# Gated linear attention and a soft mixture of experts: stages of one tile form side by side on TensorE, turns of 112 columns, and another order at the start and the end

## The chip, the cores and the metric

The program runs on one core of one Trainium2 chip. The metric is the device time of one execution in microseconds (us), the median of several runs. Everything is float32.

## The reference

```python
f = 1.0 / (1.0 + np.exp(-f_logit))
for t in range(S):                       # S = 768, for each of B = 4, H = 8, D = 48
    state = f[:, :, t, :, None] * state + np.einsum('bhd,bhe->bhde', k[:, :, t], v[:, :, t])
    y[:, :, t] = np.einsum('bhd,bhde->bhe', q[:, :, t], state)
x = y.transpose(0, 2, 1, 3).reshape(B * S, H * D)              # 3072 x 384
logits = x @ phi                                               # 32 slots, 4 for each of 8 experts
d = softmax of logits over the 3072 tokens;   slot_input = d.T @ x
slot_out[e] = np.maximum(slot_input[e] @ w1[e], 0.0) @ w2[e]   # 384 -> 1024 -> 384
c = softmax of logits over the 32 slots;      out = c @ slot_out
```

## The kernel before

**Units.** The attention is cut into 12 units (NU): 6 chunks of 128 time steps, for each two batches at a time. A unit holds 16 heads, two beside each other on the partitions (rows 0 to 47 and 64 to 111), so eight head pairs of 128 columns; `w` is 0 or 1 for the first or last four of them. Unit u carries a state on to unit u + 2.

For a unit, ACT makes exp(-f) and ln(1 + ...) in place (`d_exp`, `d_ln`, L179 to L184), DVE scans it along time (`d_scan`, L189), and ACT makes the two exponentials p and g of it (`d_p` L192, `d_g` L198; g is written over f). POOL multiplies k by g (`d_k`, L202) and q by p (`d_q`, L206). `d_pend` (L209) keeps the last column of p.

TensorE then has these stages: the turns of k (`kt`, L215, eight transposes into PC, copied by ACT in `kt_copy`, L218); the scores of each half (`scores`, L226, into PD, masked and copied by DVE in `s_mask`, L229); kv (L244, k times v into PC, to which DVE adds the state, L251, and which it scales into the next state, L254); inter (L266, state times q into PB); intra for each half (L275, v times scores into PB). ACT copies PB out (`y_copy`, L287). `x_tr` (L295) turns that into PA, and `x_copy` brings it out, the first half by ACT (L300), the second by DVE (L301). PA, PB, PC and PD are all the PSUM there is, two banks each.

**Groups.** Two units make a group g of 512 tokens: `c_lg` (L313) makes their logits in PA, `c_max` (DVE, L323) the running maximum, `c_exp` the exponential et and the copy lt (ACT), `c_tr` turns both (L337), `c_copy` (DVE, L341) brings them into el, `c_pin` (L350) multiplies et with x into the second bank of PA, and `c_join` (DVE, L354) adds it to pin.

**End.** `t_max` and `t_max2` bring the maxima of the four partition groups together, `t_psi` (L400) makes the slot inputs, `up` (L408, w1 with relu on ACT) and `turn` (L414, with a masking product on DVE, L415) run four times, `t_z` (L420) makes the sums, `c_soft` and `c_soft2` the softmax over slots on DVE, `c_ct` (L443) turns it, `down` (L448) multiplies by w2 in 16 steps for each half h of the output columns, `slot_out` and `slot_out2` (L455, L460) add up over experts and copy to s4, `combine` (L472) makes the output, copied by ACT and DVE (L475) and stored in six DMAs (L478). `flag` looks whether p and exp stayed in range; if not, a slower general part would run. `warm` (L151) is a product of ones whose result is not used.

**Order.** The order is written out by hand: `at(t, fn, ...)` gives each stage a planned time (unit length T, offsets OFF), the stages are sorted by it, and every engine runs its own in that order. Each load is issued by SP in the same order, eight at most in flight. The buffers are rings: f three, p two, k and q three, v three, x three. w1 is loaded all along, w2 into the rings of f, p, k, q and v as they come free at the end.

The forms in which TensorE is used are: scores 48 rows x 128 columns (two at once), turns 128 x 128, kv and intra 128 x 48 (two at once), inter 48 x 48 (four), lg, pin, up and down 128 x 32 (four).

## Time and profile before

| | us |
|---|---|
| timed runs | 181.41, 182.70, 182.75; median 182.7 |
| profiled execution | 180.49 |
| its span, first to last instruction | 178.8 |
| TensorE busy | 154.9 (87% of the span) |
| DVE busy | 105.0 (59%) |
| ACT busy | 92.5 (52%) |
| POOL busy | 56.9 (32%) |

The profile is that of one execution. Busy time is an average over stages: the units fill the span from about 10 to 123 us, the end the rest. Where TensorE is busy nearly all the time, its own stream of work sets the pace; where it is not, one has to look at which wait ends last. The granted clock is the share of TensorE's full 2.4 GHz that it got in a stretch; 0.5 is its lower level of 1.2 GHz. The 1.7 us between the span and the time of the execution lie outside of the instructions.

### The profile page before, as it was taken

What the parts mean: (1) busy time and instruction counts of PE and PEld (TensorE: products, weight loads), DVE (VectorE), ACT (ScalarE), POOL (GpSimd) and SP (SyncE); (2) the same over time, 40 slices, a digit from 0 to 9 for tenths busy, and PEclk for the clock granted to TensorE, in tenths of its full rate; (3) what the DMA queues carried; (4) which work ended last, traced back from release to release, by engine and by line L of the source; (5) the groups of instructions that cost most, each with busy time, mean ns of one, the idle gap of its engine ahead of it and who ended that gap; (6) DMA issues with size and microseconds to landing.
All of it is one profiled execution on the core that took longest, in us unless ns stands there. A gap on an engine that the chain in (4) does not pass through costs nothing. (4 is left out here: it accounts for less than half of the span.)

```text
span 178.8 us, 5442 instructions
## 1 busy us (share of the span) xinstructions
PE 154.9 (87%) x2396; PEld 116.5 (65%) x2396; DVE 105.0 (59%) x140; ACT 92.5 (52%) x156; POOL 56.9 (32%) x43
## 2 busy tenths in 40 slices
PE   7858599999999999999999999999898899898600
PEld 7747498878787878877787787767533346464400
DVE  6588266678787777777869677273424822225420
ACT  5965991858767595939493956402303112023410
POOL 2324846290909072725555374500000000000000
PEclk9999756999999999999999999999999999999955
DMA  4999999999299958999797948199978992009690
GB/s 140 324 406 414 408 410 409 391 312 405 67 414 396 391 201 262 369 415 330 279 363 231 341 143 343 28 408 421 419 313 282 423 423 110 5 5 368 266 406 33
DMA packets 12849, 53.97 MB, mean 302 GB/s; under 512 B 1425, under 2 KB 1553, under 8 KB 12817
## 3 DMA queue, kind: packets, MB, share of 16 engines
q1 hardware_dynamic: 12816, 53.55, 78.3%
q8 instruction: 20, 0.33, 0.7%
q14 instruction: 13, 0.10, 0.2%
HBM read 48.82 MB, written 4.72 MB: 300 GB/s over the span
## 5 line engine op out<-in xcount | busy, mean ns | idle before, releaser
L206 POOL TENSOR_TENSOR arena<-arena 128x1024 f32<-128x1024 f32 (+1 forms) x12 | 26.3, 2189 | 45.2 <-ACT arena L192 40.1
L229 DVE TENSOR_TENSOR arena<-pd,mask 128x1024 f32<-128x1024 f32 x24 | 29.3, 1223 | 18.6 <-PE pd L226 18.4
L202 POOL TENSOR_TENSOR arena<-arena 128x1024 f32<-128x1024 f32 (+1 forms) x14 | 29.5, 2112 | 11.5 <-DMA arena<-in_k_dram 5.8
L226 PE MATMUL pd<-arena 48*128 48x128 f32 x384 | 29.7, 297 | 3.2 <-DVE arena L206 2.5
L189 DVE TENSOR_TENSOR_SCAN arena<-again,arena 128x1024 f32<-128x1024 f32 (+1 forms) x14 | 29.5, 2110 | 4.7 <-ACT arena L184 4.6
L226 PEld LDWEIGHTS pd<-arena 48*128 48x128 f32 x384 | 25.0, 199 | 10.1 <-issue 5.0
L275 PE MATMUL pb<-arena 128*48 128x128 f32 x384 | 26.0, 281 | 0.0
L275 PEld LDWEIGHTS pb<-arena 128*48 128x48 f32 x384 | 20.5, 125 | 3.7 <-issue 3.5
L218 ACT COPY arena<-pc 128x768 f32<-128x768 f32 x10 | 8.0, 800 | 19.0 <-PE pc L215 19.0
L192 ACT ACTIVATE arena<-arena 128x1024 f32<-128x1024 f32 (+1 forms) x14 | 13.2, 940 | 2.7 <-DVE arena L189 2.7
L181 ACT ACTIVATE arena<-arena 128x1024 f32<-128x1024 f32 (+1 forms) x14 | 12.9, 924 | 2.1 <-DMA arena<-in_f_dram 2.1
L215 PE MATMUL pc<-ident,arena 128*128 128x128 f32 x80 | 11.6, 288 | 2.8 <-POOL arena L202 2.7
L295 PE MATMUL pa<-ident,arena 128*128 128x128 f32 x96 | 14.0, 292 | 0.0
L198 ACT ACTIVATE arena<-arena 128x1024 f32<-128x1024 f32 (+1 forms) x14 | 13.1, 936 | 0.5
L184 ACT ACTIVATE arena<-arena 128x1024 f32<-128x1024 f32 (+1 forms) x14 | 13.1, 934 | 0.4
L287 ACT COPY arena<-pb 128x1024 f32<-128x1024 f32 x11 | 11.2, 1017 | 2.3 <-PE pb L275 2.3
L300 ACT COPY arena<-pa 128x384 f32<-128x384 f32 x12 | 5.7, 478 | 12.8 <-PE pa L295 12.8
L215 PEld LDWEIGHTS pc<-ident,arena 128*128 128x128 f32 x80 | 8.8, 145 | 5.1 <-POOL arena L202 3.8
L295 PEld LDWEIGHTS pa<-ident,arena 128*128 128x128 f32 x96 | 11.0, 148 | 1.6 <-issue 0.4
L266 PE MATMUL pb<-arena 48*48 48x128 f32 x320 | 10.9, 274 | 0.0
L448 PE MATMUL pd<-arena 128*32 128x192 f32 x144 | 9.2, 330 | 1.0 <-DVE sob L455 0.6
L301 DVE COPY arena<-pa 128x384 f32<-128x384 f32 x12 | 6.7, 558 | 5.7 <-ACT arena L300 5.7
(123 smaller groups left out, 195.9 us busy)
## 6 DMA issues: line engine op xcount, KB each, us to landing
wr<-in_w_dram SPq DMA_DIRECT2D x23, 768.0 KB, 7.7
arena<-in_w_dram SPq DMA_DIRECT2D x9, 768.0 KB, 9.7
arena<-in_k_dram SPq DMA_DIRECT2D x12, 512.0 KB, 5.5
arena<-in_q_dram SPq DMA_DIRECT2D x12, 512.0 KB, 6.8
arena<-in_f_dram SPq DMA_DIRECT2D x10, 512.0 KB, 7.1
arena<-in_v_dram SPq DMA_DIRECT2D x12, 384.0 KB, 6.2
out_dram<-wr SPq DMA_DIRECT2D x6, 768.0 KB, 4.2
arena<-in_f_dram SPq DMA_DIRECT2D x4, 256.0 KB, 4.8
```

Of the source, the lines that this page charges most:

```text
L181: nc.scalar.activation(cols(R("f", u), h), cols(R("f", u), h), AF.Exp, scale=-1.0, accum_out=a)
L184: nc.scalar.activation(cols(R("f", u), h), cols(R("f", u), h), AF.Ln, bias=1.0)
L189: nc.vector.tensor_tensor_scan(t, cols(again, h), t, 0.0, op0=ALU.mult, op1=ALU.add)
L192: nc.scalar.activation(cols(R("p", u), h), cols(R("f", u), h), AF.Exp, scale=-1.0)
L198: nc.scalar.activation(cols(G(u), h), cols(R("f", u), h), AF.Exp)
L202: (eng or nc.gpsimd).tensor_tensor(t, t, cols(G(u), h), op=ALU.mult)
L206: (eng or nc.gpsimd).tensor_tensor(t, t, cols(R("p", u), h), op=ALU.mult)
L215: nc.tensor.transpose(PC[:, a // 4, 128 * (a % 4) : 128 * (a % 4) + 128], kq[:, a], ident)
L226: nc.tensor.matmul(PD[:, r, 128 * p : 128 * p + 128], kq[rs, 4 * w + p], qq[rs, 4 * w + p], start=True, stop=True)
L229: nc.vector.tensor_tensor(heads(R("sc", w), L), PD.rearrange("p r (a t) -> p (r a) t", t=L), mask.unsqueeze(1).broadcast_to([128, 8, L]), ...
L275: nc.tensor.matmul(ys[o : o + D, 4 * w + p], vb(u, 4 * w + p, r ^ w), sc[:, r, p], start=u < 2 and p == 0, stop=p == 3, skip_group_check=True,
L295: nc.tensor.transpose(PA[:, w, 128 * p : 128 * p + 128], xTs[u][:, w, p], ident)
```

## The change

The planned unit length and all offsets are new, and so is the sequence: what follows is the order on the engines. The diff without the table and lists of order:

```diff
+W = 64 + 48
-    NF, NP_, NK, NQ, NVB, NX = 3, 2, 3, 3, 3, 3
+    NF, NP_, NK, NQ, NVB, NX = 3, 2, 3, 3, 2, 4
...
-            nc.tensor.transpose(PC[:, a // 4, 128 * (a % 4) : 128 * (a % 4) + 128], kq[:, a], ident)
+            nc.tensor.transpose(PC[:, a // 4, 128 * (a % 4) : 128 * (a % 4) + W], kq[:W, a], ident[:W, :W])
...
+    def SP(u, w):
+
+        return PA if u == 0 and w else PD
...
-                nc.tensor.matmul(PD[:, r, 128 * p : 128 * p + 128], kq[rs, 4 * w + p], qq[rs, 4 * w + p], start=True, stop=True)
+                nc.tensor.matmul(SP(u, w)[:, r, 128 * p : 128 * p + 128], kq[rs, 4 * w + p], qq[rs, 4 * w + p], start=True, stop=True)
...
-            nc.vector.tensor_copy(t[:, 1], PB[:, 1])
+
+    def y_last(u):
+        t = xTs[u].rearrange("p n a t -> p n (a t)")
+        nc.scalar.copy(t[:, 1, :256], PB[:, 1, :256])
+        nc.vector.tensor_copy(t[:, 1, 256:], PB[:, 1, 256:])
...
-                nc.tensor.transpose(PA[:, w, 128 * p : 128 * p + 128], xTs[u][:, w, p], ident)
+                nc.tensor.transpose(PA[:, w, 128 * p : 128 * p + W], xTs[u][:W, w, p], ident[:W, :W])
...
-        return (PA if g < NV - 1 else PC)[:, 1]
+        return PB[:, 0] if g < NV - 1 else PC[:, 1]
...
-    FIN = [(PA, PC), (PB, PA), (PC, PB)]
+    FIN = [[(PA, PC), (PB, PA), (PC, PB)], [(PA, PB), (PC, PD), (PA, PB)]]
...
-        items = [(t_psi,), (warm, 1), (up, 0, 0), (c_exp, NV - 1, (1,)), (c_tr, NV - 1, (1,)), (c_copy, NV - 1, (1,)), (c_soft,), (up, 0, 1), (turn, 0, 0)]
-        items += [(c_soft2,), (up, 1, 0), (turn, 0, 1), (t_z,), (up, 1, 1), (turn, 1, 0)]
+        items = [(t_psi,), (c_exp, NV - 1, (1,)), (t_zs,), (up, 0, 0), (up, 0, 1), (c_tr, NV - 1, (1,)), (turn, 0, 0), (c_copy, NV - 1, (1,))]
+        items += [(up, 1, 0), (turn, 0, 1), (t_z,), (c_soft,), (up, 1, 1)]
...
+        items += [(down, 0, *STEPS[x]) for x in range(8)]
+        items += [(turn, 1, 0), (turn, 1, 1), (c_soft2,), (flag,)]
+        for x in range(8, 16):
+            items.append((down, 0, *STEPS[x]))
+        items += [(slot_out, 0), (c_ct, 0), (c_ct, 1), (flag_2,)]
+        items += [(down, 1, *STEPS[x]) for x in range(2)]
...
-        (y_copy, NU - 1), (warm, 2), (c_lg, NV - 1), (x_tr, NU - 1), (c_max, NV - 1), (x_copy, NU - 1), (warm, 2),
-        (c_exp, NV - 1, (0,)), (c_tr, NV - 1, (0,)), (c_copy, NV - 1, (0,)), (t_max,), (warm, 1), (t_max2,),
-        (c_pin, NV - 1), (c_join, NV - 1), (warm, 2),
+        (y_last, NU - 1), (c_lg, NV - 1), (x_tr, NU - 1), (c_max, NV - 1), (c_exp, NV - 1, (0,)), (t_max,), (c_tr, NV - 1, (0,)),
+        (c_copy, NV - 1, (0,)), (x_copy, NU - 1), (t_max2,), (warm, 1), (c_pin, NV - 1), (c_join, NV - 1), (warm, 1),
```

Of y of the last unit, the first bank is now copied by ACT behind the first intra stage, and the second in two halves by `y_last`. `t_zs` makes zs, which was the first line of `t_z`; `flag_2` holds what was the second half of `flag`.

**The first place** is the middle of the program, units 4 and 5. On TensorE before (L226 scores, L244 kv, L266 inter, L295 turns of x, L275 intra, L313 logits, L215 turns of k, L337 turns of et and lt):

```order
L226 MATMUL pd<-arena 128x128 x8
L244 MATMUL pc<-arena 48x48 x16
L266 MATMUL pb<-arena 48x128 x16
L226 MATMUL pd<-arena 128x128 x8
L295 MATMUL pa<-ident,arena 128x128 x8
L275 MATMUL pb<-arena 48x128 x8
L313 MATMUL pa<-arena,phs 32x128 x16
L215 MATMUL pc<-ident,arena 128x128 x8
L275 MATMUL pb<-arena 48x128 x8
L226 MATMUL pd<-arena 128x128 x8
L337 MATMUL pa<-ident,et 128x128
L337 MATMUL pa<-ident,lt 128x128
```

On TensorE now, the same place (L232 scores, L217 turns of k, L305 turns of x, L362 pin, L325 logits, L272 inter, L250 kv, L281 intra, L349 turns of et and lt):

```order
L232 MATMUL pd<-arena 128x128 x8
L217 MATMUL pc<-ident,arena 128x112 x8
L305 MATMUL pa<-ident,arena 128x112 x8
L232 MATMUL pd<-arena 128x128 x8
L362 MATMUL pa<-arena,el 32x384 x4
L325 MATMUL pa<-arena,phs 32x128 x16
L272 MATMUL pb<-arena 48x128 x16
L250 MATMUL pc<-arena 48x48 x16
L281 MATMUL pb<-arena 48x128 x16
L232 MATMUL pd<-arena 128x128 x8
L217 MATMUL pc<-ident,arena 128x112 x8
L305 MATMUL pa<-ident,arena 128x112 x8
```

The turns of k stand with those of x (and in odd units with those of et and lt, which now go to PB), pin stands with the logits, kv with both intra stages; a unit is finished before the next begins.

On ACT before, in such a unit (L287 y, L192 p, L198 g, L181 exp, L184 ln, L209 last column of p, L300 x, L218 copy of the turned k):

```order
L287 COPY arena<-pb 128x1024
L192 ACTIVATE arena<-arena 128x1024
L198 ACTIVATE arena<-arena 128x1024
L181 ACTIVATE arena,check<-arena 128x1024
L184 ACTIVATE arena<-arena 128x1024
L209 COPY check<-arena 128x8
L300 COPY arena<-pa 128x384
L218 COPY arena<-pc 128x768
```

On ACT now (L293 y, L194 p, L220 copy of the turned k, L311 x, L200 g, L211, L183 exp, L186 ln):

```order
L293 COPY arena<-pb 128x1024
L194 ACTIVATE arena<-arena 128x1024
L220 COPY arena<-pc 128x768
L311 COPY arena<-pa 128x384
L200 ACTIVATE arena<-arena 128x1024
L211 COPY check<-arena 128x8
L183 ACTIVATE arena,check<-arena 128x1024
L186 ACTIVATE arena<-arena 128x1024
```

The copies of k and x have moved between p and g of the next unit. DVE, which before had the scan behind the copy of x, now has it behind the second mask and both state products.

**The second place** is unit 2 on DVE. Before (L229 mask, L254 state, L301 x, L189 scan):

```order
L189 SCALAR_TENSOR_TENSOR arena<-again,arena 128x1024
L229 TENSOR_TENSOR arena<-pd,mask 128x1024
L254 TENSOR_TENSOR arena<-pc,check 128x384
L229 TENSOR_TENSOR arena<-pd,mask 128x1024
L301 COPY arena<-pa 128x384
L189 SCALAR_TENSOR_TENSOR arena<-again,arena 128x1024
L229 TENSOR_TENSOR arena<-pd,mask 128x1024
```

Now (L235 mask, L191 scan, L313 x, L260 state):

```order
L235 TENSOR_TENSOR arena<-pd,mask 128x1024
L191 SCALAR_TENSOR_TENSOR arena<-again,arena 128x512 x2
L313 COPY arena<-pa 128x384
L235 TENSOR_TENSOR arena<-pd,mask 128x1024
L260 TENSOR_TENSOR arena<-pc,check 128x384
L191 SCALAR_TENSOR_TENSOR arena<-again,arena 128x1024
L235 TENSOR_TENSOR arena<-pd,mask 128x1024
```

The first row is now the first mask of unit 1; unit 2 is scanned in halves behind it, and the scan of unit 3 stands ahead of the first mask of unit 2 (last two rows). In the start besides, all four half products of k and q of unit 0 are on DVE (those of k were on POOL), units 1 and 2 have their products in halves on POOL, q ahead of k, both scores of unit 0 stand together, and the loads of k and f of the next units have moved ahead of v.

**The third place** is the end on TensorE. Before (L400 psi, L408 up, L337 turn of lt, L414 turn, L420 sums, L448 down):

```order
L400 MATMUL pd<-wd,pin 32x32 x12
L151 MATMUL pc<-ones 128x128
L408 MATMUL pa<-wr,et 32x512 x12
L337 MATMUL pc<-ident,lt 128x128
L408 MATMUL pa<-wr,et 32x512 x12
L414 MATMUL pb<-ident,arena 128x128 x4
L408 MATMUL pc<-wr,et 32x512 x12
L414 MATMUL pb<-ident,arena 128x128 x4
L420 MATMUL pd<-small,same 128x1
L408 MATMUL pc<-wr,et 32x512 x12
L414 MATMUL pb<-ident,arena 128x128 x4
L448 MATMUL pd<-arena 32x192 x12
```

Now (L412 psi, L420 up, L349 turn of lt, L426 turn, L434 sums, L462 down, L457 `c_ct`):

```order
L412 MATMUL pd<-wd,pin 32x32 x12
L420 MATMUL pa<-wr,et 32x512 x24
L349 MATMUL pc<-ident,lt 128x128
L426 MATMUL pb<-ident,arena 128x128 x4
L420 MATMUL pc<-wr,et 32x512 x12
L426 MATMUL pb<-ident,arena 128x128 x4
L434 MATMUL pd<-small,same 128x1
L420 MATMUL pc<-wr,et 32x512 x12
L462 MATMUL pd<-arena 32x192 x32
L426 MATMUL pb<-ident,arena 128x128 x8
L462 MATMUL pd<-arena 32x192 x32
L457 MATMUL pc<-ident,el 128x128 x6
```

The first two up stages stand together, the last two turns stand together in the middle of the first 16 down steps, and `c_ct` behind them. Two instead of four down steps of the second half stand ahead of `slot_out2`, and the others are spread 4, 4, 4, 2 instead of 4, 3, 3, 2 from there on.

## Rows read from the trace of the kernel before

**Rows 1.** The view that gives each engine's busy time (number of instructions) in stretches of the span, with granted clock, share of the DMA engines and GB/s; us from the span's start.
```profile
18.00:22.00 4.00, 2.20 (x12) 1.63 (x14) 0.65 (x1) 3.77 (x7) 3.54 (x3) 0.72 1.02 406
22.00:27.00 5.00, 4.99 (x63) 4.41 (x61) 3.37 (x3) 4.52 (x7) 2.14 (x1) 0.50 1.02 412
27.00:32.00 5.00, 5.00 (x43) 4.30 (x44) 3.75 (x3) 0.92 (x2) 2.53 (x2) 0.70 1.03 411
...
51.00:70.00 19.00, 18.66 (x336) 15.09 (x334) 14.48 (x18) 13.63 (x23) 9.40 (x4) 1.00 0.87 331
```

**Rows 2.** TensorE's timeline in the middle, most of a period of two units (start, us from the first start to the last end, line, what, number of instructions, [idle before <- releaser]; a stage's 8 matmuls of two passes are 16 instructions, a turn is one).
```profile
51.32 1.16 PE L226 MATMUL pd<-arena 48*128 48x128 f32 x16
52.41 0.92 PE L244 MATMUL pc<-arena 128*48 128x48 f32 x32
53.27 1.09 PE L266 MATMUL pb<-arena 48*48 48x128 f32 x32
...
57.74 1.08 PE L313 MATMUL pa<-arena,phs 128*32 128x128 f32 x32 [0.26 <-DVE arena L301]
58.76 1.09 PE L215 MATMUL pc<-ident,arena 128*128 128x128 f32 x8
59.78 1.08 PE L275 MATMUL pb<-arena 128*48 128x128 f32 x16
60.79 1.16 PE L226 MATMUL pd<-arena 48*128 48x128 f32 x16
...
64.23 0.85 PE L350 MATMUL pa<-arena,el 128*32 128x384 f32 x8
...
70.28 1.16 PE L226 MATMUL pd<-arena 48*128 48x128 f32 x16
```

**Rows 3.** TensorE's timeline again: two intra stages that stand together and the score stage behind them; then two short cuts out of one stage of turns, for the pace of its instructions.
```profile
105.06 1.95 PE L275 MATMUL pb<-arena 128*48 128x128 f32 x32
106.94 1.16 PE L226 MATMUL pd<-arena 48*128 48x128 f32 x16
...
47.42 0.71 PE L295 MATMUL pa<-ident,arena 128*128 128x128 f32 x5
...
47.53 0.38 PE L295 MATMUL pa<-ident,arena 128*128 128x128 f32 x2
```

**Rows 4.** Groups of instructions by line and form, of TensorE's weight loads (number, busy us, mean ns of one, idle before).
```profile
L215 PEld LDWEIGHTS pc<-ident,arena 128*128 128x128 f32 x80 | 8.8, 145 | 5.1 <-POOL arena L202 3.8 <-issue 1.2
L244 PEld LDWEIGHTS pc<-arena 128*48 128x48 f32 x320 | 8.6, 131 | 1.4 <-issue 0.5 <-ACT arena L181 0.2 <-DMA arena<-in_q_dram 0.2
```

**Rows 5.** The same view, of DVE and ACT.
```profile
L229 DVE TENSOR_TENSOR arena<-pd,mask 128x1024 f32<-128x1024 f32 x24 | 29.3, 1223 | 18.6 <-PE pd L226 18.4
...
L189 DVE TENSOR_TENSOR_SCAN arena<-again,arena 128x1024 f32<-128x1024 f32 x10 | 24.7, 2466 | 4.1 <-ACT arena L184 4.1
...
L192 ACT ACTIVATE arena<-arena 128x1024 f32<-128x1024 f32 x10 | 10.7, 1067 | 0.8 <-DVE arena L189 0.8
...
L218 ACT COPY arena<-pc 128x768 f32<-128x768 f32 x10 | 8.0, 800 | 19.0 <-PE pc L215 19.0
...
L300 ACT COPY arena<-pa 128x384 f32<-128x384 f32 x12 | 5.7, 478 | 12.8 <-PE pa L295 12.8
...
L301 DVE COPY arena<-pa 128x384 f32<-128x384 f32 x12 | 6.7, 558 | 5.7 <-ACT arena L300 5.7
...
L251 DVE TENSOR_TENSOR pc<-pc,arena 128x384 f32<-128x384 f32 x8 | 4.5, 561 | 0.3
```

**Rows 6.** ACT's timeline in one unit, from exp to the op behind ln.
```profile
64.41 1.04 ACT L181 ACTIVATE arena<-arena 128x1024 f32<-128x1024 f32 x1
...
65.58 1.06 ACT L184 ACTIVATE arena<-arena 128x1024 f32<-128x1024 f32 x1
66.54 0.19 ACT L209 COPY check<-arena 128x8 f32<-128x8 f32 x1
```

**Rows 7.** Timelines of the start, of DVE (first row) and of TensorE.
```profile
8.78 2.40 DVE L206 TENSOR_TENSOR arena<-arena 128x512 f32<-128x512 f32 x2 [1.45 <-ACT check L209]
...
10.68 1.16 PE L226 MATMUL pd<-arena 48*128 48x128 f32 x16 [2.47 <-DVE arena L206]
...
17.91 0.66 PE L215 MATMUL pc<-ident,arena 128*128 128x128 f32 x4 [0.91 <-POOL arena L202]
20.37 1.12 PE L215 MATMUL pc<-ident,arena 128*128 128x128 f32 x4 [1.80 <-POOL arena L202]
...
41.93 1.16 PE L226 MATMUL pd<-arena 48*128 48x128 f32 x16
```

**Rows 8.** TensorE's timeline from the end of the last unit's intra stages to the last combine.
```profile
122.58 0.71 PE L151 MATMUL pc<-ones 128*128 128x128 f32 x4
...
131.04 2.78 PE L408 MATMUL pa<-wr,et 128*32 128x512 f32 x24
134.78 0.33 PE L337 MATMUL pc<-ident,lt 128*128 128x128 f32 x1 [0.95 <-ACT lt L333]
...
142.55 0.38 PE L420 MATMUL pd<-small,same 128*128 128x1 f32 x2 [0.85 <-DVE small L419]
...
155.92 0.59 PE L460 MATMUL pd<-sob,same 128*128 128x192 f32 x2
...
169.07 0.43 PE L472 MATMUL pb<-s,ct 32*128 32x192 f32 x2 [0.59 <-ACT wr L475]
```

More of the change, by code (lines that the diff above doesn't have):

```diff
@@ L551, in gla_soft_moe_kernel @@
     done0 = ("kt", "ktok", "sc0", "sc1", "mask0", "mask1", "intra0", "intra1", "kv", "st", "s2", "inter", "y")
[L552 to L553 removed]
+    for h in range(2):
+        for x, (fn, t) in enumerate(((d_scan, 1.5), (d_p, 2.9), (d_g, 3.0), (d_q, 2.95), (d_k, 3.05))):
+            at(T + t + 0.2 * h, fn, 2, h)
     for u in range(NU):
@@ L573, in gla_soft_moe_kernel @@
         for key, fn in (("lg", c_lg), ("mx", c_max), ("et", c_exp), ("tr", c_tr), ("el", c_copy), ("pin", c_pin), ("join", c_join)):
-            at(z + o[key], fn, g)
+            at(z + o[key] - (T if g == NV - 2 and key in ("pin", "join") else 0), fn, g)
     at(-3, load_phi)
```

71 lines of the change are left out of this document (32 added, 39 removed).

## The prediction

> **What bounds the kernel now.** I read the table of stretches first. In 51 to 70 us, one period of two units, TensorE is busy for 18.66 of 19.00 us at the full granted clock, DVE for 14.48, ACT for 13.63, POOL for 9.40 [rows 1]. So in the middle only TensorE's own stream counts. The same view shows one place where it isn't full speed: the granted clock is 0.72, 0.50 and 0.70 of full in the stretches 18:22, 22:27 and 27:32 [rows 1]. At the two levels 1.0 and 0.5 that is 2.24 + 5.00 + 3.00 = 10.2 us at 1.2 GHz.
>
> Next, TensorE's timeline of one period. From the first score stage of one unit to that of the next but one (51.32 to 70.28) it takes 18.96 us [rows 2], and 19 stages stand in it. Start to start, a score stage (half of the heads) takes 1.09, kv 0.86, lg 1.02, a turn of eight 1.02, an intra stage 1.01; the pin stage lasts 0.85 with the tail of its last product (0.79 without, as I take it); of these rows only lg shows a wait, 0.26 [rows 2].
>
> **The change, part by part.**
>
> *Stages of one form together.* Two intra stages that already stand together start 1.88 apart from the next stage (105.06 to 106.94) [rows 3], where two apart take 2 x 1.01 [rows 2]: a join saves about 0.15. Within a stage of turns, five take 0.71 and two 0.38, so one follows the next by 0.11 [rows 3]; 8 x 0.11 = 0.88 of the 1.02, the rest is the border. After the change the period has 11 groups instead of 19 stages (score; turns of k, x and, every other unit, of et and lt; score; pin with lg; inter; kv with both intra). Eight joins are 1.2 us.
>
> *Turns of 112 columns.* If a turn's pace is that of its moving columns, 0.11 x 16/128 = 0.013 goes from each, 8 x 4 = 32 a period: 0.43. What speaks against: the weights stay 128 columns wide. Their loads take 145 ns for a turn and 131 for the 48 columns of kv [rows 4]: 80 columns more cost 14 ns, so a load is mostly fixed latency, and I take the moving columns as the pace. Bounds: 0 and 0.43.
> The Trainium skill, "TensorE: Matmul & The Clock Gate", section "LDWEIGHTS (loading the stationary operand)", says that a load takes its columns divided by 1.2 ns; by that 128 columns are 107 ns, the load sets the pace and cutting the moving columns gives nothing. By that rule the 0.43 would be 0. No run here shows a turn with fewer columns yet.
>
> TensorE alone would then need 18.96 - 1.2 - 0.4 - 0.3 (the wait of lg) = 17.0 a period, 7.7 in a unit with the turns of et and lt (odd units) and 9.2 in one with pin and lg (even units).
>
> *What the new order ties to it.* Here I leave TensorE. In the new order ACT has, per unit: p of the next unit, copy of kt, copy of x, g, exp, ln, y; DVE has mask, x copy, mask, the two state products, then the scan of the unit after next. So p waits for the scan, the x copies wait for p, and in an even unit pin and lg wait for the x copies (same bank, PA); then inter, kv, the state products, and the next scan. In order, with an op on ACT followed by the next 0.1 before it ends (ln starts at 65.58 and the next op at 66.54, for an op of 1.06) [rows 5, 6]: p 0.96, kt copy 0.70, x on ACT 0.48, x on DVE 0.56, pin 0.79, lg 0.87 (joined), inter 1.02 (as lg), kv 0.86, state 0.56 twice, scan 2.47 [rows 2, 5] = 9.8, and eight handovers of about 0.05 (estimate) = 10.2. In an odd unit the longer way is scan, mask 1.22, score 1.09, inter 1.02, kv 0.86, state 1.12, scan 2.47 = 7.8, with handovers 8.1; by ACT alone (p, kt copy, x, g 0.96, exp 1.17 [rows 6], ln 1.06, scan) it is the same within 0.3. Together 18.3; the scan's mean holds some that ran beside POOL products on the same tiles, now less so, and I take 18.1. Bounds: 17.0 (TensorE alone) and 18.9 (nothing gained). So about 1.1 us of the 1.9 that TensorE saves per period is expected to come back as waits for the x copies and the mask in even units.
>
> *Start, to the first score stage of unit 3.* Before, this stage starts at 41.93; there are waits of 0.91 and 1.80 for POOL's k [rows 7], and the half clock follows them. Now DVE makes all four half products of unit 0. The q product starts at 8.78 and the two halves took 2.40 beside POOL's [rows 7]; alone a half is some 0.65 (half of a mask's 1.22 [rows 5]), so the first score starts at about 9.5 instead of 10.68 (bounds 9.4 and 10.7). The second score goes to PA and doesn't wait for the mask. TensorE's work to unit 3 at full clock is 6.0 + 6.5 + 8.5 = 21.0 (unit 0: two scores, turns, three value stages; unit 1 adds turns of x; unit 2 lg and inter, all from rows 2 less the joins). That gives 30.5 without a wait. New waits: in unit 2 the mask stands on DVE behind the scan of unit 3. From the end of unit 2's ln to the second score of unit 2 there are two half scans (2.4), the last half p and g (1.2), exp 1.17, ln 1.06, scan 2.47, mask 1.22 and handovers, about 10.5 [rows 5, 6]; TensorE has 7.7 of work in that time. So some 3 are lost there, and I add 1.4 in unit 0 (masks between half scans) and 0.9 in unit 1 (k halves from POOL, mask). Sum 5.4, bounds 3 and 8: unit 3 starts at 35.9, which is 6.0 earlier. The loads of the first units are reordered but not late: v of unit 0 is still ahead of unit 1's q.
>
> *Middle.* 35.9 + 8.6 (unit 3, with four small copies ahead of its mask) + 3 x 18.1 + 8.8 (unit 10, no kv and no turns of k) + 7.3 (unit 11) = 114.9 where the intra stages of the last unit end, against 122.58 before [rows 8]: 7.7 gained.
>
> *End.* From there to the first up stage it took 8.46 (122.58 to 131.04) [rows 8]. Now y comes out of its bank in halves, the maximum is passed on ahead of the x copies, and six of the eight warm-up products go: I count 1.8 (bounds 0.8 and 2.5; the pin stage still waits for both x copies). From up to the first total over slots it took 24.88 (131.04 to 155.92), with waits of 0.95 and 0.85 [rows 8]. Both go, since lt is copied earlier and zs is made earlier; joining up with up and turn with turn saves 1.4 net of a wait for the last turn's product: 3.2. Two more down steps come behind it, 0.65. Other banks for the last combine take away waits like the one of 0.59 [rows 8], but the stores behind it follow each other at the pace of the DMA, so 0 (bounds 0 and 1.2). End: 4.4.
>
> *Buffers.* v has two instead of three; its load can start only when the unit two before is done; kv comes a whole unit (9) and its own place in the unit (5) later, so some 14 us cover it, and I count nothing. If the cover were gone, kv would wait in each unit, and the intra stages, y and the next turns of x behind it.
>
> **Sum.** 7.7 + 4.4 = 12.1 off the profiled execution's 180.5 (span 178.8): 168.4. The three timed runs lie 0.9 to 2.3 above that execution; I forecast 169 for the median.
>
> **The rivals.**
> - *Start goes cold again.* TensorE still waits 3 us in unit 2, in pieces up to about 1.5; before, 0.91 and 1.80 close together [rows 7] were followed by half clock. Price: 10.2 us at half clock cost some 4.5 before, since TensorE was busy for 4.99 of 5.00 in it [rows 1]; here some is covered by waits: 3.5. Then 172.5.
> - *Only TensorE counts.* ACT and DVE keep ahead, the period is 17.0 and unit 10 loses its waits: 3 x 1.1 + 1.0 less, 165. For it: ACT and DVE have 4 to 5 us of free time per period [rows 1]. Against it: the chain above.
> - *The change doesn't do what it says to the stream:* turns keep their pace and the joins give half. The period becomes 18.6 by TensorE, and start and end give 1.5 less: 172.
> - *Slower.* The clock falls in the middle too, because each even unit now has TensorE waiting about 1 us. At half clock an even unit's 9.2 us of work takes some 17, 7 to 8 more. Two such units eat the 12 to 14 us gained, three make it slower, near 187. Against: 51:70 with a wait of 0.26 kept the clock [rows 1, 2], and only waits as long as 0.91 and 1.80 came ahead of a fall.
>
> **How the numbers follow.** Forecast (167 to 171) 0.55; cold start 0.18; TensorE alone 0.14; stream unchanged 0.05; slower 0.04; the rest, 0.04, is several small losses near no change. The range 164 to 174 takes in the first four. A measurement of this kernel tells about 1% from no change. Faster by over 1%: 0.91; within 1%: 0.05; slower by over 1%: 0.04.
>
> **What would show it.** A timeline of a period with 18.0 to 18.3 from score to score of the next but one, longer in even units (about 10) than in odd ones (about 8), with TensorE's pin stage waiting for the DVE copy of x and the second score for the mask; turns 0.095 apart (0.11 if the load sets the pace); unit 3's first score near 36; granted clock 1.0 at 20 to 35 us; first up stage 6.7 after the last intra stage. It is wrong if the period is under 17.4 or over 18.7, or if unit 3 starts later than 38.

## The result and the profile after

The changed kernel takes 175.16 us (median of 4 runs, 174.31 to 177.31), the kernel before beside it 182.06; the ratio is 0.9615 with a 95% interval of 0.9517 to 0.9713. It is faster, but by 7 us and not by the 13 of the forecast, and 175.2 lies above the range's 174. The profiled execution is the slowest of the four, 177.31 (span 175.6): its clock was low for longer in the start than in the second profile of this kernel (below). The ratio is formed from each kernel's undisturbed runs, so that it need not be the quotient of the medians.

**The period.** TensorE's timeline in the changed kernel, one period of two units, in the columns of [rows 2]:

```profile
49.00 1.16 PE L232 MATMUL pd<-arena 48*128 48x128 f32 x16
50.09 0.98 PE L217 MATMUL pc<-ident,arena 112*128 112x112 f32 x8
50.91 0.93 PE L305 MATMUL pa<-ident,arena 112*128 112x112 f32 x8
51.89 1.16 PE L232 MATMUL pd<-arena 48*128 48x128 f32 x16
53.58 0.85 PE L362 MATMUL pa<-arena,el 128*32 128x384 f32 x8 [0.53 <-DVE arena L313]
...
58.86 1.16 PE L232 MATMUL pd<-arena 48*128 48x128 f32 x16
...
61.86 1.16 PE L232 MATMUL pd<-arena 48*128 48x128 f32 x16
63.78 1.09 PE L272 MATMUL pb<-arena 48*48 48x128 f32 x32 [0.76 <-DVE el L353]
...
67.40 0.38 PE L232 MATMUL pd<-arena 48*128 48x128 f32 x2
```

49.00 to 67.40 is 18.40 (before 18.96 [rows 2], forecast 18.1): 9.86 in the even unit, 8.54 in the odd one. TensorE waits 0.53 for VectorE's half of the x copy (L313), as forecast, and 0.76 for el, the copy of the turned weights (L353), which the forecast doesn't have. Without the two waits it is 17.11, where 17.0 was forecast. Eight turns take 0.82 from their first to the next stage (50.09 to 50.91). What el's copy is queued behind is seen in the timeline of ScalarE and VectorE ahead of that wait:

```profile
60.68 1.06 ACT L194 ACTIVATE arena<-arena 128x1024 f32<-128x1024 f32 x1 [0.68 <-DVE arena L191]
61.64 0.78 ACT L220 COPY arena<-pc 128x768 f32<-128x768 f32 x1
...
62.32 0.48 ACT L311 COPY arena<-pa 128x384 f32<-128x384 f32 x1
...
62.84 0.56 DVE L313 COPY arena<-pa 128x384 f32<-128x384 f32 x1 [1.13 <-ACT arena L311]
63.31 0.41 DVE L353 COPY el<-pb 128x256 f32<-128x256 f32 x1
```

The exponential p (L194) waits for the scan (L191), the copies of the turned k (kt, L220) and of x (L311) follow it on ScalarE, VectorE's x copy waits for that, and el comes behind. The second score of units 4 to 9 waits for no mask, though the forecast had such a wait in even units; it stands in units 3 and 10 only (0.77 and 0.72).

**The start.** First the busy times and the granted clock in stretches, in the columns of [rows 1], then TensorE's timeline from the first score stage to that of unit 3:

```profile
11.00:18.00 7.00, 7.00 (x78) 6.25 (x78) 4.79 (x5) 5.70 (x12) 3.78 (x3) 0.51 1.04 412
18.00:24.00 6.00, 6.00 (x112) 5.43 (x108) 4.43 (x6) 4.79 (x10) 2.33 (x3) 1.00 1.02 414
24.00:31.00 7.00, 4.66 (x60) 3.67 (x54) 5.38 (x5) 4.45 (x8) 4.37 (x4) 1.00 1.02 409
31.00:38.50 7.50, 6.81 (x108) 5.75 (x110) 2.71 (x4) 5.51 (x11) 5.28 (x11) 0.54 0.86 342
```

```profile
10.06 1.20 PE L232 MATMUL pd<-arena 48*128 48x128 f32 x16 [2.77 <-DVE arena L208]
11.26 2.08 PE L232 MATMUL pa<-arena 48*128 48x128 f32 x16
...
26.24 1.16 PE L232 MATMUL pd<-arena 48*128 48x128 f32 x16
...
31.69 2.08 PE L232 MATMUL pd<-arena 48*128 48x128 f32 x16 [1.90 <-DVE arena L235]
...
40.44 1.16 PE L232 MATMUL pd<-arena 48*128 48x128 f32 x16
```

The clock was at its lower level (1.2 GHz) twice, behind the wait of 2.77 for the first score and behind the 1.90 for unit 2's mask (the stretches at 0.51 and 0.54). Unit 3 starts at 40.44, not at 35.9. Its own length is 8.56, as forecast (8.6). The scan that unit 2's mask stands behind took 3.26, where the forecast had set 2.47; what made it long is told at the end.

**The end**, TensorE's timeline from the last intra stage's end to the second total over slots:

```profile
120.42 0.41 PE L325 MATMUL pc<-arena,phs 128*32 128x128 f32 x4
...
127.31 2.78 PE L420 MATMUL pa<-wr,et 128*32 128x512 f32 x24 [0.39 <-DVE small L430]
130.89 2.78 PE L420 MATMUL pa<-wr,et 128*32 128x512 f32 x24 [0.79 <-ACT arena L421]
...
135.41 2.78 PE L420 MATMUL pc<-wr,et 128*32 128x512 f32 x24 [1.05 <-DVE el L353]
...
145.83 0.63 PE L426 MATMUL pb<-ident,arena 128*128 128x128 f32 x4 [0.94 <-DVE arena L427]
...
152.13 0.59 PE L474 MATMUL pd<-sob,same 128*128 128x192 f32 x2
161.59 0.59 PE L474 MATMUL pd<-sob,same 128*128 128x192 f32 x2 [0.70 <-DVE sob L469]
```

First up 6.89 behind the intra stages (8.46 before [rows 8], forecast 6.66). From first up to the total over slots 24.82, against 24.88 before [rows 8]: nothing of the forecast's 3.2 came. The waits of 0.95 and 0.85 [rows 8] are gone, and 0.79, 1.05 and 0.94 stand in their place.

So the forecast's 168.4 is missed in the profiled execution by 4.5 (start), 0.9 (three periods), 0.3 (units 10 and 11, way to the first up) and 3.1 (first up to the total over slots): 168.4 + 8.8 = 177.2, and 177.31 was measured.

### The profile page after: what moved, and what is told of

Its sections match the earlier page's. It is cut to its first block, busy times and chain, and to the rows that moved or that the text cites. A ratio compares the mean times of both kernels' runs of the same rounds, so it can differ in the third digit from the quotient of the medians.

```text
span 175.6 us, 5429 instructions
## 1 busy us (share of the span) xinstructions
PE 145.7 (83%) x2384; PEld 114.0 (65%) x2384; DVE 105.1 (60%) x143; ACT 91.7 (52%) x159; POOL 54.5 (31%) x43
## 4 chain that ended last, share of the span: by engine, by line
PE 44%; DVE 28%; ACT 13%; issue 4%; DMA 4%; SPq 1%; DVEq 0%; ACTq 0%
DVE arena L191 11%; PE pb L272 6%; PE pc L250 5%; PE pd L462 4%; ACT arena L194 4%; DMA arena<-in_q_dram 4%; PE pd L232 4%; PE pa L420 3%; PE pc L420 3%; PE pa L325 3%; PE pa L362 3%; DVE arena L235 3%; PE pb L281 3%; DVE pc L257 3%; ACT arena L220 2%
## 5 line engine op out<-in xcount | busy, mean ns | idle before, releaser
L208 POOL TENSOR_TENSOR arena<-arena 128x1024 f32<-128x1024 f32 (+1 forms) x13 | 27.0, 2076 | 56.7 <-ACT arena L194 39.1
L232 PE MATMUL pd<-arena 48*128 48x128 f32 x368 | 27.7, 291 | 6.3 <-DVE arena L235 3.4
L235 DVE TENSOR_TENSOR arena<-pd,mask 128x1024 f32<-128x1024 f32 x23 | 27.8, 1210 | 4.0 <-PE pd L232 4.0
L191 DVE TENSOR_TENSOR_SCAN arena<-again,arena 128x1024 f32<-128x1024 f32 (+1 forms) x15 | 28.7, 1919 | 2.5 <-ACT arena L186 2.4
L232 PEld LDWEIGHTS pd<-arena 48*128 48x128 f32 x368 | 23.1, 193 | 10.6 <-DVE arena L235 5.5
L204 POOL TENSOR_TENSOR arena<-arena 128x1024 f32<-128x1024 f32 (+1 forms) x13 | 26.5, 2038 | 0.0
L281 PE MATMUL pb<-arena 128*48 128x128 f32 x384 | 24.4, 280 | 0.6 <-DVE arena L235 0.6
L281 PEld LDWEIGHTS pb<-arena 128*48 128x48 f32 x384 | 21.0, 126 | 1.6 <-DVE arena L235 0.9
L293 ACT COPY arena<-pb 128x1024 f32<-128x1024 f32 x11 | 11.1, 1011 | 14.5 <-PE pb L281 14.5
L194 ACT ACTIVATE arena<-arena 128x1024 f32<-128x1024 f32 (+1 forms) x15 | 13.3, 884 | 8.2 <-DVE arena L191 8.2
L183 ACT ACTIVATE arena<-arena 128x1024 f32<-128x1024 f32 (+1 forms) x14 | 13.1, 937 | 2.7 <-DMA arena<-in_f_dram 2.7
L272 PE MATMUL pb<-arena 48*48 48x128 f32 x320 | 11.8, 288 | 2.3 <-DVE el L353 2.3
L200 ACT ACTIVATE arena<-arena 128x1024 f32<-128x1024 f32 (+1 forms) x15 | 13.4, 892 | 0.3
L186 ACT ACTIVATE arena<-arena 128x1024 f32<-128x1024 f32 (+1 forms) x14 | 13.1, 936 | 0.4
L272 PEld LDWEIGHTS pb<-arena 48*48 48x48 f32 x320 | 9.1, 127 | 4.8 <-DVE el L353 2.9
L313 DVE COPY arena<-pa 128x384 f32<-128x384 f32 x12 | 6.6, 553 | 9.1 <-ACT arena L311 9.1
L427 DVE TENSOR_TENSOR arena<-pb,emask 128x512 f32<-128x512 f32 x4 | 2.8, 691 | 14.8 <-PE pb L426 14.8
L305 PE MATMUL pa<-ident,arena 112*128 112x112 f32 x96 | 11.3, 261 | 0.3 <-ACT arena L293 0.2
L217 PE MATMUL pc<-ident,arena 112*128 112x112 f32 x80 | 10.8, 280 | 0.5 <-POOL arena L204 0.5
L250 PEld LDWEIGHTS pc<-arena 128*48 128x48 f32 x320 | 9.1, 136 | 1.8 <-issue 1.7
L305 PEld LDWEIGHTS pa<-ident,arena 112*128 112x128 f32 x96 | 9.6, 141 | 0.8 <-ACT arena L293 0.6
L250 PE MATMUL pc<-arena 128*48 128x48 f32 x320 | 10.1, 221 | 0.0
```

The lines of the kernel that those rows point to most:

```text
L183: nc.scalar.activation(cols(R("f", u), h), cols(R("f", u), h), AF.Exp, scale=-1.0, accum_out=a)
L191: nc.vector.tensor_tensor_scan(t, cols(again, h), t, 0.0, op0=ALU.mult, op1=ALU.add)
L194: nc.scalar.activation(cols(R("p", u), h), cols(R("f", u), h), AF.Exp, scale=-1.0)
L200: nc.scalar.activation(cols(G(u), h), cols(R("f", u), h), AF.Exp)
L204: (eng or nc.gpsimd).tensor_tensor(t, t, cols(G(u), h), op=ALU.mult)
L208: (eng or nc.gpsimd).tensor_tensor(t, t, cols(R("p", u), h), op=ALU.mult)
```

## The experiments

The kernels of one group ran on one chip, with the kernel before: the first four, the next four, the two after them (three edits, scan in halves), the two with the early logarithm, and the last alone.

**The changed kernel again**, as the measure for the next three.

> The changed kernel once more, as the measure for the others on this chip. If its 174 to 177 us come from its order of work, and the spread of its runs from how often TensorE's granted clock fell to half in the start, this run shows 174.0 to 176.0, the period again 18.4, unit 3's first score at 38 to 41, and the end from first up to the second output stage of half 0 again 24.8. If the profiled execution was a chance, the first score of unit 3 stands near 36 and the time below 172.

175.68 us (174.24 to 177.35), 0.9659 [0.9579, 0.9739] of before. Period 18.41, first up to slots 24.83, unit 3 at 38.87; the second stay at the lower clock was shorter in this profile. Period and end are the same in both profiles, and what differs is the clock in the start.

**el ahead of the x copy on VectorE.**

```diff
-    lg=T + 3.9, mx=T + 5.4, et=T + 5.8, tr=2 * T + 2.75, el=2 * T + 2.9, pin=3 * T + 3.85, join=3 * T + 5.2,
+    lg=T + 3.9, mx=T + 5.4, et=T + 5.8, tr=2 * T + 2.7, el=2 * T + 2.75, pin=3 * T + 3.85, join=3 * T + 5.2,
```

> The odd unit's copy of the turned weights (el, L353) is put ahead of VectorE's half of the x copy. Theory A: the 0.76 us that the state product (inter, L272) waits in the odd unit is the place of that copy behind the x copy (0.475 us from start to start); it falls to about 0.3, five times, the period from 18.4 to 17.9, the time by 2 us to about 173. Rival: the loop through scan, exponential, copies and scores sets the period at 18.1 to 18.4 whatever the order of these two; inter's wait goes, but pin or the next unit's mask waits as much longer, the period stays within 0.15 of 18.4 and the time within 0.7 us.

173.61 us, 0.9556 [0.9492, 0.9621], 2.1 below the changed kernel on the same chip. Theory A: the odd unit takes 7.71 (57.08 to 64.79) and inter doesn't wait. But then the next unit's second score waits for the mask:

```profile
57.08 1.16 PE L232 MATMUL pd<-arena 48*128 48x128 f32 x16
...
61.17 1.09 PE L272 MATMUL pb<-arena 48*48 48x128 f32 x32
...
64.79 1.16 PE L232 MATMUL pd<-arena 48*128 48x128 f32 x16
...
68.05 1.16 PE L232 MATMUL pd<-arena 48*128 48x128 f32 x16 [0.41 <-DVE arena L235]
```

The period is 17.6 once and then 17.95: of the 0.76, 0.41 came back as a wait for the mask, which stands behind the scan. That scan now starts before GpSimd's product of k is done, and takes 2.64 where it took 2.28:

```profile
62.36 2.37 POOL L204 TENSOR_TENSOR arena<-arena 128x1024 f32<-128x1024 f32 x1
64.24 2.64 DVE L191 TENSOR_TENSOR_SCAN arena<-again,arena 128x1024 f32<-128x1024 f32 x1
```

**The scan ahead of the two state operations.**

```diff
-    exp=4.45 - 2 * T, ln=5.6 - 2 * T, scan=7.1 - 2 * T, p=1.0 - T, dq=2.05 - T, g=3.3 - T, dk=4.4 - T, pend=4.35 - T,
+    exp=4.45 - 2 * T, ln=5.6 - 2 * T, scan=6.15 - 2 * T, p=1.0 - T, dq=2.05 - T, g=3.3 - T, dk=4.4 - T, pend=4.35 - T,
```

> VectorE's scan stands ahead of the two state operations (L257, L260) instead of behind them, nothing else. Theory A, by the chain of the prediction (scan, exponential p, kt copy, x copy on ScalarE, x copy on VectorE, pin): scan starts 1.6 us earlier in the even unit and 2 us in the odd one, p then waits for the y copy alone, the x copies come 0.4 to 0.5 earlier, pin's 0.53 goes and inter's 0.76 shrinks to about 0.3: period about 17.4, time down by 3 to 4 us to about 171.5. Rival: ScalarE's order (y copy, p, kt copy, x copy) or the state, now later, holds the stream: kt waits for the state's read of its bank and the period stays 18.2 to 18.6, the time within 1 us of the changed kernel's.

176.24 us, 0.9704 [0.9632, 0.9775], 0.6 above the changed kernel, and the two intervals overlap. The rival: pin no longer waits and inter only 0.18, but kt waits 0.90 to 1.01 for the state operation L260, and the period stays 18.3 to 18.45. VectorE's timeline shows why the state is late:

```profile
64.81 2.45 DVE L191 TENSOR_TENSOR_SCAN arena<-again,arena 128x1024 f32<-128x1024 f32 x1 [1.15 <-ACT arena L186]
67.19 0.53 DVE L257 TENSOR_TENSOR pc<-pc,arena 128x384 f32<-128x384 f32 x1
67.75 0.56 DVE L260 TENSOR_TENSOR arena<-pc,check 128x384 f32<-128x384 f32 x1
```

The scan waits 1.15 for the logarithm (L186) on ScalarE, and the state behind it with it. The edit moves the scan of unit 3 too: unit 2's kt then waits 3.61 for the state, and unit 3 starts at 39.90.

**Tiles and order of the end.**

```diff
-    UPB = [PA[:, 0], PA[:, 1], PC[:, 0], PC[:, 1]]
+    UPB = [PA[:, 0], PC[:, 0], PA[:, 1], PC[:, 1]]
...
-        items = [(t_psi,), (c_exp, NV - 1, (1,)), (t_zs,), (up, 0, 0), (up, 0, 1), (c_tr, NV - 1, (1,)), (turn, 0, 0), (c_copy, NV - 1, (1,))]
-        items += [(up, 1, 0), (turn, 0, 1), (t_z,), (c_soft,), (up, 1, 1)]
+        items = [(t_psi,), (c_exp, NV - 1, (1,)), (t_zs,), (c_tr, NV - 1, (1,)), (c_copy, NV - 1, (1,)), (up, 0, 0), (up, 0, 1), (turn, 0, 0)]
+        items += [(up, 1, 0), (turn, 0, 1), (t_z,), (c_soft,), (up, 1, 1), (turn, 1, 0)]
...
-        items += [(turn, 1, 0), (turn, 1, 1), (c_soft2,), (flag,)]
+        items += [(turn, 1, 1), (c_soft2,), (flag,)]
```

> Only the end is touched: the four products up go to the tiles PA, PC, PA, PC instead of PA, PA, PC, PC, the turn of lt and its copy stand ahead of the first up, and the third turn of the hidden layer directly behind the last up. Theory A: the waits of 0.79 (second up, for the copy of the first from the other bank of its tile), 1.05 (third up) and 0.94 (fourth turn) are dependencies by whole tile of two banks; with the tiles alternating they fall to under 0.3 together, the 24.8 us from first up to the second output stage of half 0 become 22 to 23, and the time falls by 2 to 2.8 us. Rival: the copies' engines themselves (ScalarE's four relu and VectorE's turns and softmax) set the pace, the waits move to the next up or turn, and the stretch stays within 0.5 of 24.8.

172.17 us, 0.9483 [0.9418, 0.9549], 3.5 below the changed kernel. TensorE's timeline:

```profile
124.67 2.78 PE L420 MATMUL pa<-wr,et 128*32 128x512 f32 x24
127.26 2.76 PE L420 MATMUL pc<-wr,et 128*32 128x512 f32 x24
...
130.54 2.78 PE L420 MATMUL pa<-wr,et 128*32 128x512 f32 x24
...
139.99 0.66 PE L426 MATMUL pb<-ident,arena 128*128 128x128 f32 x4
...
146.32 0.59 PE L474 MATMUL pd<-sob,same 128*128 128x192 f32 x2
```

Theory A, and more than it: none of the three waits is left, and first up to slots is 21.65, the 21.7 of the forecast. The three edits ran together. That a product waited for a reader of the other bank of its tile is read from the releasers and was not run apart: for the second up it is the copy L421 of the first up, which had written PA's bank 0, while the second writes bank 1; for the third up (PC's bank 0) the copy of the turned lt out of bank 1; for the fourth turn (PB's bank 1) the masking product of the third out of bank 0.

**Unit 2's mask ahead of the scan of unit 3**, with kt and x copies ahead of unit 3's p on ScalarE.

```diff
-            at(z + o[key], fn, u, *args)
+            at({(3, "scan"): 2 * T + 1.2, (3, "p"): 2 * T + 2.85, (3, "dq"): 2 * T + 2.9}.get((u, key), z + o[key]), fn, u, *args)
```

> Only the start is touched: VectorE takes the mask of unit 2's first score ahead of the scan of unit 3, and ScalarE the kt and x copies ahead of unit 3's exponential p. Theory A: the 1.90 us that unit 2's second score waits for the mask, standing behind the scan of 3.1 to 3.3 us, is what made unit 3 late; it goes, sc1 of unit 2 stands at most 0.3 behind the x turns, unit 3's first score comes 2 to 3 us earlier (35 to 36 where the clock does not fall, 37 to 38 where it does), and the time falls by 1.5 to 3 us. Rival: unit 3's products q and k on GpSimd, now a microsecond later, hold its first score, which stays within 1 us of where it was (38 to 39), and the time within 0.8 us.

172.58 us, 0.9589 [0.9486, 0.9692]; the changed kernel took 175.2 and 175.7 on other chips. The median is 2.6 to 3.1 lower, and 2.1 lower than that of the next kernel (174.71) on the same chip; the ratios to the kernel before overlap, so it is the trace that bears out theory A. TensorE's timeline:

```profile
24.73 1.16 PE L232 MATMUL pd<-arena 48*128 48x128 f32 x16
...
28.50 1.16 PE L232 MATMUL pd<-arena 48*128 48x128 f32 x16
...
35.34 0.93 PE L232 MATMUL pd<-arena 48*128 48x128 f32 x11 [0.77 <-POOL arena L204]
```

The 1.90 is gone and the clock is at its full level from 8 to 86 us; unit 3 starts at 35.34, and in it is a wait of 0.77 for GpSimd, on which the rival had counted.

**Turns of 128 columns again.**

```diff
-W = 64 + 48
+W = 128
```

> The turns go back from 112 to 128 columns, nothing else. Theory A, the loop through scan, exponential and copies sets the period and TensorE has waits to spare (0.53 in the even unit, 0.76 in the odd one): the 16 turns of a unit cost 0.22 us more, the waits shrink by as much to about 0.31 and 0.54, the period stays 18.4 and the time within 1 us of the changed kernel's (some turns at start and end count). Rival, the term of the prediction (0.43 us a period off TensorE's work, and so off the time): the period goes to 18.8 and the time up by 2 us or more. By a third view, weight loads set the pace of a turn and the columns nothing: the turns themselves stay 0.095 us apart.

174.71 us, 0.9685 [0.9590, 0.9781]: within 1 us of the changed kernel, theory A. TensorE's timeline of a period:

```profile
46.53 1.16 PE L232 MATMUL pd<-arena 48*128 48x128 f32 x16
47.62 1.09 PE L217 MATMUL pc<-ident,arena 128*128 128x128 f32 x8
48.55 1.04 PE L305 MATMUL pa<-ident,arena 128*128 128x128 f32 x8
...
51.12 0.85 PE L362 MATMUL pa<-arena,el 128*32 128x384 f32 x8 [0.44 <-DVE arena L313]
...
61.32 1.09 PE L272 MATMUL pb<-arena 48*48 48x128 f32 x32 [0.55 <-DVE el L353]
...
64.95 1.16 PE L232 MATMUL pd<-arena 48*128 48x128 f32 x16
```

The period is 18.42. Eight turns take 0.93 instead of 0.82, and the waits shrink (0.44 and 0.55 for 0.53 and 0.76): 16 columns cost 0.014 a turn, and the kernel doesn't feel it. (The rows of what is turned go from 112 to 128 with the columns; the two weren't run apart.)

**The x turns and copies ahead of kt.**

```diff
-    xt=T + 1.95, xe=T + 2.8,
+    xt=T + 1.04, xe=T + 1.9,
-    lg=T + 3.9, mx=T + 5.4, et=T + 5.8, tr=2 * T + 2.75, el=2 * T + 2.9, pin=3 * T + 3.85, join=3 * T + 5.2,
+    lg=T + 3.9, mx=T + 5.4, et=T + 5.8, tr=2 * T + 1.07, el=2 * T + 1.85, pin=3 * T + 3.85, join=3 * T + 5.2,
```

> In every unit the x turns stand ahead of the kt turns on TensorE and the x copies ahead of the kt copy on ScalarE; the turns of et and lt come right behind the x turns, and el's copy ahead of VectorE's x copy. The x copies then no longer stand behind the kt copy (0.68 us). Theory A (the tail of the loop, from p to pin, is what TensorE waits for): pin's 0.53 goes, inter's 0.76 too, the period comes to 17.4 to 17.7, held by the wait of the second score for the mask behind the scan (0.4 in the even unit), and the time falls by 3 to 4 us. Rival: the scan itself, not what follows p, sets the pace through the mask, and the period stays at the 17.95 that el's copy alone gave; the time falls by some 2 us.

169.99 us (169.34 to 170.32), 0.9434 [0.9353, 0.9514]. Theory A: neither pin nor inter waits; the period is 17.15 once and then 17.7, with 0.29 to 0.42 for the mask in the even unit. Those waits stand behind scans of 2.55 and 2.64, which start beside GpSimd's product of k as in the kernel with el first; in the period of 17.15 the scan takes 2.28 and nothing waits. The start gained as well (unit 3 at 35.12, the clock full): the x turns now cover the wait for GpSimd's k.

**The same, and the scan ahead of the state.** The edits of the last and of the third kernel together.

> The kernel with the x turns first, and the scan ahead of the two state operations as well. With kt one stage later, the 0.98 that kt waited for the state's read of its bank is covered by the x turns (0.82). Theory A: both arms of the loop are then shorter than TensorE's own 17.1 us a period, the period comes to 17.1 to 17.3 and the time 1 to 2 us below that of the x turns first alone. Rival: VectorE's own order (scan, two state operations, mask) is the bound at the passage from the odd to the even unit, the second score waits 0.5 or more for the mask, and the period is not below that of the x turns first alone.

175.03 us, 0.9659 [0.9517, 0.9800]. Theory A fell: kt waits 0.68 to 0.70 for the state and the period is 18.2, 0.5 above that of the x turns first alone. Most of the 5.0 us by which the time is longer is the start's, though: there kt waits 1.68 for the state, the clock falls, and unit 3 begins at 39.10 instead of 35.12.

**Three edits together**: x turns first, the end's tiles, unit 2's mask first.

> Three of the edits tried apart stand together: the x turns and copies ahead of kt, the four products up alternating between two tiles, and unit 2's mask ahead of the scan of unit 3. If the gains are of separate places they add: the x turns first alone gave 170.0 with unit 3's first score at 35.1; the end is worth 3.1 more, the start 0.5 to 1.5 more: 165.5 to 166.5, the period 17.4 to 17.7 as before. Rival: the new start moves work of GpSimd and ScalarE under the x copies and unit 3 begins no earlier; 167 to 168.

167.38 us (166.49 to 168.36), 0.9208 [0.9149, 0.9268]: below the kernel before, the changed one and all others here, but as the rival has it. Unit 3 starts at 35.10, no earlier than with the x turns first alone (35.12), so that the mask-first edit gives nothing on top of it. The end's gain adds: from first up to slots it is 21.66 against 24.82 in the kernel with the x turns first.

**The scan in halves around the state**, in that kernel.

```diff
+            if key == "scan" and u > 3:
+                at(z + 6.15 - 2 * T, d_scan, u, 0)
+                at(z + o[key], d_scan, u, 1)
+                continue
```

> As the kernel with the three edits, and the scan in two halves, the first ahead of the two state operations and the second behind them. Theory A: with the x copies out of the loop, what is left of its wait is the mask behind scan on VectorE (0.3 to 0.4 us in the even unit, 1.2 in unit 10), which idles 0.72 us before the state operations while the whole scan ahead of them held them up by 1.5; a half fits the gap: the period comes to 17.1 to 17.3 and the time 1.5 to 2.5 us below that of the three edits alone. Rival: a half of 1.14 us ahead of the state is still longer than the gap, kt or the mask waits as much, and the time stays within 0.7 us.

174.32 us, 0.9592 [0.9535, 0.9649], 7 slower. Theory A fell, and the rival is too mild: in the odd unit the first half waits 1.69 for the logarithm, and the mask stands behind all of it (the second score waits 1.26). At the full clock the period is 17.75 and then 18.89 (17.15 and 17.70 in the kernel with three edits). The third is 20.17, because the clock fell at 86 us, and it fell again at 106 us, in unit 10; of the 7 us some 3 are these two stays (an estimate: 20.17 less 18.89, and unit 10, which is 2.4 longer with 0.7 more of waiting).

**The logarithm a unit earlier**, with the scan ahead of the state, once in the changed kernel and once in that with three edits.

```diff
+            if u > 4 and key in ("exp", "ln", "scan"):
+                at(z + dict(exp=6.9 - 3 * T, ln=7.0 - 3 * T, scan=6.15 - 2 * T)[key], fn, u)
+                continue
```

> The changed kernel with the scan ahead of the two state operations, and from unit 5 on with the two operations on ScalarE that make the scan's input (exponential L183 and logarithm L186) a unit earlier, ahead of a y copy. Theory A: the scan put ahead lost because the logarithm in the odd unit ends only 1.15 us after VectorE is free, so that the state waited behind a scan that waited for ScalarE (p, copies, g, exponential, logarithm, scan, p is the loop); with the logarithm early the scan starts right behind the mask, kt no longer waits (0.98 before), and the period comes to 17.2 to 17.5, pin and inter within 0.2 of no wait; the time 170 to 171.5. Rival: VectorE's order is the bound by itself, a scan of 2.28 us ahead of the state holds kt or the mask wherever its input comes from; the period stays 18.0 to 18.4 and the time within 1 us of 175.

> The kernel with the three edits (x turns first, end tiles, unit 2's mask first; 167.4), and from unit 5 on the scan ahead of the state operations and the exponential and logarithm a unit earlier. Theory A as for the changed kernel alone: TensorE's own work of 17.1 us is then the period (17.1 to 17.3 against 17.4 to 17.7), the wait of 1.2 in unit 10 goes, and the time is 1.5 to 2.5 us lower, 165 to 166. Rival: VectorE's order is the bound, the second score of the even unit waits 0.7 or more, period 18, and the time is 169 or more.

177.74 us, 0.9821 [0.9714, 0.9928], and 175.41 us, 0.9685 [0.9604, 0.9766]: the first no faster than the changed kernel, the second clearly slower than that with three edits; theory A fell twice. The periods are 18.7 to 19.0 and 17.8 to 19.1. The wait for the logarithm is gone, yet kt waits as long as ever (1.03 to 1.19, and 0.67 to 0.68). In the second the x turns of the odd unit also wait, 0.76 to 0.96, for the y copy that now stands behind the early logarithm; in unit 3 that wait is 2.08, and the clock is low from 37 to 47 us. VectorE and GpSimd in the first of the two, and TensorE's kt:

```profile
60.60 2.38 POOL L204 TENSOR_TENSOR arena<-arena 128x1024 f32<-128x1024 f32 x1
61.42 3.71 DVE L191 TENSOR_TENSOR_SCAN arena<-again,arena 128x1024 f32<-128x1024 f32 x1
...
66.23 0.98 PE L217 MATMUL pc<-ident,arena 112*128 112x112 f32 x8 [1.03 <-DVE arena L260]
```

The scan takes 3.71 instead of 2.28. It starts while GpSimd's product of k runs (60.60 to 62.98): 1.56 us of it, and 1.43 is what it takes longer.

**The same without that product.** From unit 5 on the product of k with the decay is left out, in the first of the two kernels.

```diff
+            if u > 4 and key == "dk":
+                continue
```

> The changed kernel with the logarithm early and the scan ahead of the state operations, and from unit 5 on without the product of k with the decay on GpSimd (this part of the computation is left out). Theory A: the scan ahead of the state lost because it then ran beside that product, 3.7 to 3.9 us against 2.28 where it ran alone, an excess (1.4 to 1.6) that is nearly the time for which the two overlapped (1.56 to 1.73); without the product the odd unit's scan takes 2.28, kt waits less than 0.2 for the state (1.03 to 1.19 before), and the period from unit 5 on is 17.2 to 17.6. Rival: the scan is long there for another reason (its input just written, the mask before it), stays at 3.5 or more, and the period stays 18.4 to 19.0.

Period 17.50 from unit 6 on (67.67, 85.17, 102.67), theory A. The scan right behind the mask, by VectorE's timeline:

```profile
65.05 2.28 DVE L191 TENSOR_TENSOR_SCAN arena<-again,arena 128x1024 f32<-128x1024 f32 x1
```

The turns of k don't wait for the state; inter waits 0.43 for el, as it must with the old place of el. The 174.2 us (0.9534 [0.9420, 0.9648]) are not set against the others, since a part of the work is left out and in the profile the clock is low twice in the start (unit 3 at 40.35).

## Why the prediction was right or wrong, step by step

Two steps failed: the end, where the sum took 3.2 off and nothing came, and the clock in the start, which the sum put at nothing and which cost 3.9 in the profiled execution. By its own sign, "unit 3 starts later than 38", the forecast is wrong.

**Stages of one form together: right.** TensorE without waits needs 17.11 a period; 17.0 was forecast.

**Turns of 112 columns: right in size, and worth nothing here.** A turn is 0.014 cheaper (0.93 against 0.82 for eight), 0.013 was forecast. The forecast said itself that the loop, not TensorE, would set the period, and the run with 128 columns shows it: 18.42 against 18.40. The rule of the Trainium skill, "TensorE: Matmul & The Clock Gate", section "LDWEIGHTS (loading the stationary operand)", by which a load takes its columns divided by 1.2 ns (107 for 128), isn't borne out as the pace of a turn: with the weights 128 wide in both, a turn took 0.116 with 128 moving columns and 0.1025 with 112.

**The period: right in mechanism in the even unit, wrong in the odd one, 0.3 too short.** The even unit took 9.86, with pin waiting for the x copy as forecast (10.2). The term that was mis-sized is the odd unit, 8.54 for 8.1. The step behind it, that "in an odd unit the longer way is" scan, mask, score, inter, kv, state and the next scan, doesn't hold: the way was p, kt copy, both x copies, el, inter. That el's turn had moved to PB, the bank of inter, stands in the diff; that its copy is queued behind VectorE's x copy and that inter then waits for it was overlooked. Putting el first gave 0.45 a period, and taking the kt copy out of the way (x first) the rest.

**Where the loop can be cut** the forecast didn't say, and the expectations here got it half wrong. Its tail, from p to pin and inter, can be: 18.4 became 17.7. Its head, the scan, gained nothing in the five kernels that put it (or a half) earlier: first it waits for the logarithm, and with that early, it starts beside GpSimd's product. Only without that product did the period come to 17.50; an order that keeps the product and moves it away from the scan was not run.

**The start: work and waits together were right, the clock was not.** In the runs where the clock was full, first score to unit 2's first score is 14.66 (mask-first kernel, 10.07 to 24.73), and from there to unit 3, with the changed order on VectorE, 11.78 (128 columns, 26.19 to 37.97): 26.4, and 26.4 was forecast (9.5 to 35.9). In the profiled execution the two are 16.18 and 14.20, 1.5 and 2.4 longer; in the second profile of this kernel they are 16.30 and 12.73, 1.6 and 1.0 longer. This is the rival "start goes cold again", priced at 3.5 and met at 3.9; its chance of 0.18 was too low: at least one fall stands in each of the seven profiles whose start up to unit 2's mask is in the changed kernel's order. The forecast set its 3 us in unit 2 "in pieces up to about 1.5"; the piece was 1.90, behind a scan of 3.26 that was set at 2.47. That the 26.4 comes out to the digit is luck: in the two stretches taken for it the waits are 4.3 (0.8, 0.8 and 2.7 in units 0, 1 and 2) where 5.4 were forecast, and the rest is 22.1 for 21.0.

**The end: the step that failed is "Both go", from which the 3.2 follow.** The old waits went, and new ones of 2.8 us together took their place, since the order put the second up, the third up and the fourth turn each directly behind a late reader of the other bank of their tile; that the dependency goes by the whole tile is read from the releasers. With tiles and order changed the 3.2 are there (21.65). To the first up (6.89 for 6.66) and with the two downs more and the last combines (23.5 from the first total to the span's end, 0.6 more than the 22.9 before [rows 8]; 0.65 was forecast) it was right, and so were the buffers: kv never waits for v.

With the cold start alone the range would have held the time (172.5); with the end's 3.1 and the period's 0.9 on top it could not. Even the lowest of the four runs (174.31) lies above the range. One price doesn't add up in itself: in the rival "Slower", three units of 7 to 8 us more on top of the forecast are 190 or more, not 187; the clock didn't fall in the middle of the changed kernel, and nothing else rests on it.

## What to carry to other kernels

A stage that is tied into a loop over several engines can gain nothing from cheaper instructions (here 0.43 us of columns gave 0.02 a period); find which end of the loop can be moved, and look at what the earlier place would run beside. Where dependencies go by a tile of several banks, let products that follow each other alternate between tiles, and ask of every wait that is removed who is queued one step further. A wait has to be priced with the clock behind it: unit 2's mask behind the scan cost 1.2 by itself (11.78 from unit 2 to unit 3, of which turns of 128 columns are 0.2, against 10.61 with the mask first, both at the full clock), and where the clock fell, 1.0 to 2.4 more.
